# Queries of two batches loaded eight tokens to a partition, turned with the key tile, and ordered by VectorE

## The chip, the cores and the metric

One Trainium2 chip; the program runs on one of its cores. The metric is the time of one execution on the device, in microseconds, and the median over several runs is compared. Times inside an execution come from one profiled execution, counted from its first instruction.

## What is computed

Attention over four batches of eight heads with 768 tokens of 64 numbers, and after it a two-layer network. Each token attends to the tokens less than 16 away, and to 24 summaries, one for each block of 32 tokens: the key of a summary is the maximum over the block, its value the mean.

```python
k_sum = k.reshape(B, H, nb, block, D).max(axis=3)
v_sum = v.reshape(B, H, nb, block, D).mean(axis=3)
scores_l = scale * np.matmul(q, k.transpose(0, 1, 3, 2))
mask_l = np.abs(pos[:, None] - pos[None, :]) < window
scores_s = scale * np.einsum('bhsd,bhnd->bhsn', q, k_sum) + np.log(block)
...
out_a = np.matmul(softmax(concat(masked scores_l, scores_s)), concat(v, v_sum))
x = out_a as (3072 tokens, 512)
h = x @ w_in
return (h * sigmoid(beta * h)) @ w_out          # 512 -> 2048 -> 512
```

## The kernel before

**Stages.** The four batches are worked one after another, batch 0 in a way of its own. For a batch b from 1 on there are two stages. In the H stage sixteen steps (`h_tile`, L516) compute the hidden layer: `w_in` by the attention's output `xT`, 384 columns a matmul (L509), SiLU on ScalarE (L521) into `h_sb`. In the O stage six output tiles of 128 tokens are computed in four atoms each (`o_atom`, L534; matmuls L526) into the PSUM tiles `one[0]` and `one[1]` in turn; VectorE copies a finished tile to `o_sb` (`o_out`, L529) and SyncE stores it. While batch b is in its H stage, keys, queries and values of batch n = b + 1 are brought in; while it is in its O stage, the attention of batch n is computed between the atoms.

**Order.** Nothing plans the order: `run` (L551) calls the steps of a stage, and after each step those entries of a list whose position (a number of steps) has been reached. Each engine, and SyncE with its DMAs, does what it was given strictly in this order, so a waiting instruction holds up all behind it on that engine.

**How a batch comes in (L724 to L743).** Heads go in pairs, g = 0 to 3. Keys: loaded in the O stage before by `key_load` (L94) as 96 rows of two heads by eight tokens, so that a packet has 8 x 64 x 4 bytes = 2 KB; cast to bf16 by `key_cast` (L480), on GpSimd for pairs 0 and 2, on VectorE for 1 and 3; turned by a DMA transpose on SyncE's queue (`kq_dma`, L487) into `kT[g]`, where the tokens then lie as 8 blocks of 96, token 8r + c at column 96c + r; `windows_perm` (L223, two VectorE copies recorded at L247) cuts the overlapping windows of 96 tokens out of it into `kw[g]`, in the right order; `key_max_win` (L232) takes the block maxima, and `key_sums` (L240, GpSimd) spreads them over the windows. After that nothing reads `kT[g]` until the next batch's keys.

Queries: loaded by `hw_load` (L89) as 128 rows of two heads by six tokens that lie 128 apart, so that a packet has 64 x 4 = 256 bytes; cast by GpSimd (`kq_cast`, L472); turned by `kq_dma` into `qn[g]`, in order at once. Values: `load_v` (L101), 256 bytes a packet, cast by `v_cast` (L343) and half of them moved to other partitions by DMA (`v_odd_dma`, L354).

In the O stage `scores` (L323) multiplies `kw` and `qn` (L328), two halves of 384 queries for each pair; ScalarE takes the exponential (L335); VectorE masks it (`mask_e`, L337); `vm_all` (L384) sums the blocks of values in `one[0]` (L388) between the second and the third output tile; `av_mm` (L406) applies the weights to the values. `UNITS` (L721) gives the places: the scores of pair 0 and of the first half of pair 1 after the second atom, three more units after the sixth, pair 3 after the twelfth.

**Positions in the H stage.** Query loads at 0 and 0.1 for pairs 0 and 1, 0.7 and 1.7 for 2 and 3; key cast and turn at 0.5 + g and 0.6 + g; windows and maxima at 3.5 + g; query casts at 4.7 + g; query turns at 6.6 + 1.5g; spreads at 8 + g; values' casts at 12.6 + 1.2g. Casted keys and casted queries have four buffers each (tags `kn` and `qn` of the pool `nat`).

Of the kernel before, what the change touches and what calls it, by code (L numbers as in the profile page):

```python
# [11 lines left out]
def kernel(  # L12
# [10 lines left out]
    nc = tc.nc  # L23
    ctx.enter_context(tc.manual_schedule())
    P = 128
    f32 = mybir.dt.float32
    bf16 = mybir.dt.bfloat16
# [4 lines left out]
    B, H, S, D = q.shape  # L32
# [7 lines left out]
    J6 = S // P  # L40
# [4 lines left out]
    CK = 8  # L45
    RK = S // CK
# [11 lines left out]
    stage = ctx.enter_context(tc.tile_pool(name="stage", bufs=4))  # L58
    natp = ctx.enter_context(tc.tile_pool(name="nat", bufs=4))
# [10 lines left out]
    def pair(a, b, g):  # L70
        return a[b, 2 * g:2 * g + 2]


    stg = {}
# [11 lines left out]
    def sw_load(t, src, b, lo, hi):  # L86
        return nc.gpsimd.dma_start(out=row_view(t, b, lo, hi), in_=src[b, lo:hi].rearrange("h (p c) d -> p h (c d)", c=CS[b]))  # L87

    def hw_load(nm, src, b, g):  # L89
        f = stage.tile([P, 2, J6, D], f32, name=nm + "st", tag=nm + "st")  # L90
        stg[(nm, b, g)] = f
        nc.sync.dma_start(out=f[:], in_=pair(src, b, g).rearrange("h (j p) d -> p h j d", p=P))

    def key_load(b, g):  # L94
        f = stage.tile([RK, 2, CK * D], f32, name="kst", tag="kst")
        stg[("k", b, g)] = f
        nc.sync.dma_start(out=f[:], in_=pair(k, b, g).rearrange("h (p c) d -> p h (c d)", c=CK))

    vst = [const.tile([P, JV, D], f32, name=f"vst{g}") for g in range(G)]

    def load_v(b, g):  # L101
        src = pair(v, b, g).rearrange("h (j p) d -> p (h j) d", p=P)
        i = nc.sync.dma_start(out=vst[g][W:P, 0:JV - 1], in_=src[0:P - W])
        nc.sync.dma_start(out=vst[g][0:W, 1:JV], in_=src[P - W:P])
        return i
# [6 lines left out]
    def behind(a, b):  # L112
        tc.add_manual_dep(a.ins, b.ins.name,
                          mybir.DependencyInfo(mybir.DependencyClass.Sync, mybir.DependencyReason.DATA),
                          reason="order of loads")
# [27 lines left out]
    kT = [const.tile([P, S + 2 * W], bf16, name=f"kT{g}") for g in range(G)]  # L143
# [47 lines left out]
    qn = [const.tile([P, S], bf16, name=f"qn{g}") for g in range(G)]  # L191
# [31 lines left out]
    def windows_perm(cp, g, src, C):  # L223
        R, F, FW = S // C, QT // C, W // C
        t = kw[g][:, :, 0:NK].rearrange("p m (f c) -> p m f c", c=C)
        cs = src.ap[1][0]
        cp(t[:, 1:NT - 1], strided(src[:, :, F - FW:], [[F, NT - 2], [1, F + 2 * FW], [cs, C]]))
        e = kw[g][:, 0, W:NK]
        cp(strided(e, [[(NT - 1) * P - W, 2], [C, F + FW], [1, C]]),
           strided(src[:, :, 0:1], [[R - F - FW, 2], [1, F + FW], [cs, C]]))  # L230

    def key_max_win(g):  # L232
        nc.vector.tensor_reduce(out=km[g][:, NK:NK + nb].rearrange("p (m n) -> p m n", n=2),  # L233
                                in_=kw[g][:, :, W:W + QT].rearrange("p m (n f) -> p m n f", f=block), op=ALU.max, axis=AX.X)
# [5 lines left out]
    def key_sums(eng, g):  # L240
        eng.tensor_copy(out=kw[g][:, :, NK:NK + nb], in_=km[g][:, None, NK:NK + nb].to_broadcast([P, NT, nb]))  # L241
# [42 lines left out]
    def km_pe(g, ks):  # L284
        key_max_win(g)
        key_sums(ks, g)
# [56 lines left out]
    def v_cast(eng, g, lo=0, hi=JV):  # L343
        eng.tensor_copy(out=ve[:, g, lo:hi, 0:D], in_=vst[g][:, lo:hi])  # L344
# [9 lines left out]
    def v_odd_dma(g):  # L354
        nc.sync.dma_start(out=vo[0:QT, g, :, :], in_=ve[QT:P, g, :, :])
        nc.sync.dma_start(out=vo[QT:NK, g, 0:JV - 1, :], in_=ve[0:2 * W, g, 1:JV, :])
# [112 lines left out]

    nat = {}  # L470

    def kq_cast(eng, nm, b, g):  # L472
        t = natp.tile([P, J6, 2, D], bf16, name=nm + "n", tag=nm + "n")
        nat[(nm, b, g)] = t
        return eng.tensor_copy(out=t[:], in_=stg[(nm, b, g)].rearrange("p h j d -> p j h d"))  # L475

    last_mask = {}
    KC = [nc.gpsimd, nc.vector, nc.gpsimd, nc.vector]

    def key_cast(n, g):  # L480
        t = natp.tile([RK, CK, 2, D], bf16, name="kn", tag="kn")
        nat[("k", n, g)] = t
        i = KC[g].tensor_copy(out=t[:], in_=stg[("k", n, g)].rearrange("p h (c d) -> p c h d", c=CK))  # L483
        if g == 0 and n - 1 in last_mask:
            behind(i, last_mask[n - 1])

    def kq_dma(nm, b, g):  # L487
        t = kT[g][:, 0:S] if nm == "k" else qn[g][:]
        nc.sync.dma_start_transpose(out=t.rearrange("p (j t) -> p j t", j=CK if nm == "k" else J6),
                                    in_=nat[(nm, b, g)].rearrange("p j h d -> p (j h d)"))  # L490


    def h_begin(i, t, lo, hi):
# [57 lines left out]
    def run(main, sides):  # L551
        sides = sorted(sides, key=lambda x: x[0])
        for i, f in enumerate(main):
            f()
            while sides and sides[0][0] < i + 1:
                sides.pop(0)[1]()
        for _, f in sides:
            f()
# [83 lines left out]
    s = []  # L642
    wo = []

    def scale4(p, eng=None):
        for n in range(4 * p, 4 * p + 4):
            scale_w_out(n, eng)
# [27 lines left out]
    s = [(6, lambda: scale4(1)), (12, lambda: scale4(2)), (.5, clear_kw), (14, lambda: km_pe(0, nc.gpsimd))]  # L675
# [15 lines left out]
    def x_pe2(b, g, t):  # L691
        t = t.bitcast(bf16)[:, 0, 0:S]
        x = xn[(b, g)]
        for j in range(J6):
# [3 lines left out]
    s = [(.05, exp_table), (.15, lambda: scale4(3)), (.2, lambda: km_pe(1, nc.gpsimd)),  # L698
         (.3, lambda: km_pe(2, nc.gpsimd)), (3.52, lambda: km_pe(3, nc.gpsimd))]
# [16 lines left out]
    for g in range(G):  # L716
        s.append(((3.56, 3.561, 3.562, 3.563)[g], lambda g=g: key_load(2, g)))
# [6 lines left out]
    for b in range(1, B):  # L724
        n = b + 1
        s = []
        if n < B:
            for g in range(2):
                s.append((0 + .1 * g, lambda g=g, n=n: hw_load("q", q, n, g)))
            for g in range(G):  # L730
                s.append((.5 + g, lambda g=g: key_cast(n, g)))
                s.append((.6 + g, lambda g=g: kq_dma("k", n, g)))
                s.append((3.5 + g, lambda g=g: windows_perm(dve_cp, g, kT[g][:, 0:S].rearrange("p (c r) -> p c r", c=CK), CK)))
                s.append((3.6 + g, lambda g=g: key_max_win(g)))
                s.append((4.7 + g, lambda g=g: kq_cast(nc.gpsimd, "q", n, g)))
                s.append((8 + g, lambda g=g: key_sums(nc.gpsimd, g)))
                s.append((6.6 + 1.5 * g, lambda g=g: kq_dma("q", n, g)))
                s.append((12.6 + 1.2 * g, lambda g=g: v_cast(nc.gpsimd, g)))
                s.append((12.7 + 1.2 * g, lambda g=g: v_odd_dma(g)))
            for g in range(2):  # L740
                s.append((.7 + g, lambda g=g, n=n: hw_load("q", q, n, g + 2)))
                s.append((2.7 + g, lambda g=g: load_v(n, g)))
                s.append((6.7 + 1.5 * g, lambda g=g: load_v(n, g + 2)))  # L743
        if n + 1 < B:
            for g in range(G):
                s.append(((16.31, 16.32, 19.3, 19.31)[g], lambda g=g, n=n: key_load(n + 1, g)))
        late = [x for x in s if x[0] >= 16]
        run([lambda i=i: h_tile(b, i) for i in range(k2)], [x for x in s if x[0] < 16])
        s = [((x[0] - 16) * 1.2, x[1]) for x in late]
        if n < B:  # L750
            for j, (g, u, bg, pos, late) in enumerate(UNITS):
                s.append((pos + .01 * j, lambda n=n, g=g, u=u, bg=bg: scores(n, g, u, bg)))
                if g < G - 1:
                    s.append((late, lambda n=n, g=g, u=u: mask_e(n, g, u)))
            s.append((.05, exp_table))
            s.append((11.19, silu_table))
            av_at(n, s, [11.2, 14.1, 14.2, 14.3], [0, 1, 2, 0])
            for g in range(G):
                s.append(((11.3, 14.35, 14.4, 14.5)[g], lambda g=g: x_dma(n, g)))
            s.append((5.89, lambda: vm_all(one[0], [dve_cp] * 4)))  # L760
            s.append((8.3, lambda: spread(0)))
            s.append((8.31, lambda: spread(1)))
        main = [lambda ms=ms, a=a: o_atom(b, ms, a) for ms in range(J6 - (n == B)) for a in range(4)]
        run(main, s)
        if n == B:
            ms = J6 - 1
            for lo, hi in ((0, 256), (256, 512)):
                t = one[0 if lo else 1][:, 0]
                for kk in range(k2):
                    o_mm(ms, kk, t, lo, hi)  # L770
                o = op.tile([P, hi - lo], f32, name="o_half", tag=f"o_half{lo}", bufs=1)
                nc.vector.tensor_copy(out=o[:], in_=t[:, 0:hi - lo])
                nc.sync.dma_start(out=out_r[b * J6 + ms][:, lo:hi], in_=o[:])
# [29 lines left out]
```

## Time and profile before

| | us |
|---|---|
| median of 3 runs | 215.21 (214.99 to 216.19) |
| profiled execution | 215.1 |
| its span, first to last instruction | 213.2 |
| TensorE busy in it | 205.9 |
| VectorE, ScalarE, GpSimd busy | 109.9, 106.8, 53.8 |
| H stage of batch 1 | 76.1 to 97.1 |
| O stage of batch 1 | 97.1 to 122.2 |
| H stage of batch 2 | 122.2 to 143.0 |
| O stage of batch 2 | 143.0 to 168.2 |

The profiled execution's time is 1.9 us more than its span, for what lies before the first and after the last instruction. In the page, a row of forty digits shows the span in equal slices of 5.33 us, a digit being the busy share in tenths. The chain of waits is followed back from the last instruction, at each step to what released it; a row is start, length, engine, tile and line. A timeline row is start, length, engine, line, operation, output and inputs with their shapes, how many, and in square brackets how long the engine had been idle and what ended that. A row of the groups has, after the bar, busy time in all, mean ns of one, and after the second bar the idle time before them. A row of the windows has the stretch, its length, busy time and number of instructions for TensorE's matmuls, its weight loads, VectorE, ScalarE and GpSimd, and at the end the granted TensorE clock, the share of the DMA engines (over 1 where packets overlap) and GB/s. SyncE's queue is SPq; its lengths are those of the issue, and the landing comes later.

### The profile page before, as it was taken

How to read it: one execution, taken by the hardware profiler on the slowest of the kernel's cores; microseconds unless marked ns; L12 is line 12 of the kernel's file. 1: busy time of each engine (PE TensorE's matmuls, PEld its weight loads, DVE VectorE, ACT ScalarE, POOL GpSimd, SP SyncE). 2: the span in 40 equal slices, each digit the busy share in tenths (PEclk: the TensorE clock that was granted, in tenths of full speed). 3: DMA queues.
4: the chain of work that ended last, by engine and by line, in shares of the span. 5: the costliest groups of instructions: out<-in, count | busy, mean ns of one | idle time of the engine just before them, and what ended most of it. 6: DMA issues, size and time to landing. Idle time of an engine off the chain costs nothing.

```text
span 213.2 us, 5296 instructions
## 1 busy us (share of the span) xinstructions
PE 205.9 (97%) x2238; PEld 120.9 (57%) x2238; DVE 109.9 (52%) x252; ACT 106.8 (50%) x141; POOL 53.8 (25%) x85
## 2 busy tenths in 40 slices
PE   7879999999999999999999999999999999999993
PEld 7667766665445555565555466654554555554452
DVE  5567686298857723951898216644887100002121
ACT  2448785686767018669541057777450086640000
POOL 7947990002421203642003013443000000000000
PEclk9999999999999999999999999999999999999999
DMA  6999999999969989999579999999445500001212
GB/s 120 196 209 160 187 201 195 199 207 196 202 174 240 246 208 229 221 212 168 113 222 284 199 191 235 157 200 205 128 133 118 145 0 0 0 3 49 98 52 96
DMA packets 74534, 34.08 MB, mean 160 GB/s; under 512 B 61440, under 2 KB 70032, under 8 KB 74512
## 3 DMA queue, kind: packets, MB, share of 16 engines
q1 hardware_dynamic: 57440, 24.05, 53.4%
q0 software_dynamic: 7440, 7.34, 21.6%
q10 hardware_dynamic: 9632, 2.37, 7.6%
q8 instruction: 17, 0.28, 0.6%
q14 instruction: 5, 0.04, 0.1%
HBM read 27.37 MB, written 6.29 MB: 158 GB/s over the span
## 4 chain that ended last, share of the span: by engine, by line
PE 91%; DMA 3%; DVE 2%; POOL 1%; issue 1%; POOLq 0%; DVEq 0%
PE one L526 39%; PE big L509 29%; PE big L495 5%; PE one L501 3%; DMA qrow<-in_q_dram 3%; PE big L414 2%; PE big L328 2%; DVE qn L247 2%; PE big L501 2%; PE big L276 1%; PE big L315 1%; PE big L307 1%; PE one L388 1%; POOL krow L87 1%; PE big L260 1%
## 5 line engine op out<-in xcount | busy, mean ns | idle before, releaser
L526 PE MATMUL one<-w_out_sb,h_sb 128*128 128x512 bf16 (+1 forms) x400 | 85.8, 371 | 0.0
L521 ACT ACTIVATE h_sb<-big,beta_sb 128x768 bf16<-128x768 f32 x48 | 42.7, 901 | 48.0 <-PE big L509 48.0
L509 PE MATMUL big<-xT,w_in_sb 128*128 128x384 bf16 x384 | 63.1, 326 | 0.0
L526 PEld LDWEIGHTS <-h_sb 128*128 128x128 bf16 x400 | 38.0, 98 | 41.3 <-issue 0.2
L509 PEld LDWEIGHTS <-w_in_sb 128*128 128x128 bf16 x384 | 37.6, 98 | 25.3 <-issue 0.2
L247 DVE COPY o_sb<-one 128x512 f32<-128x512 f32 x19 | 13.1, 689 | 45.2 <-PE one L526 45.1
L335 ACT ACTIVATE e<-big,bias 128x768 bf16<-128x768 f32 x32 | 26.7, 898 | 15.8 <-PE big L328 13.7
L339 DVE TENSOR_TENSOR e<-e,mask 128x768 bf16<-128x768 bf16 x27 | 15.4, 596 | 13.6 <-ACT e L335 13.5
L247 DVE COPY kw<-kT 128x960 bf16<-128x960 bf16 (+1 forms) x16 | 10.3, 685 | 15.1 <-DMA kT<-kn 15.1
L344 POOL CAST ve<-vst 128x832 bf16<-128x832 f32 x15 | 13.5, 906 | 9.8 <-DMA vst<-in_v_dram 7.7
L475 POOL CAST qn<-qst 128x768 bf16<-128x768 f32 x8 | 6.6, 828 | 32.1 <-DMA qst<-in_q_dram 32.1
L241 POOL COPY kw<-km 128x288 bf16<-128x288 bf16 x12 | 6.9, 581 | 25.6 <-DVE km L233 25.6
L441 DVE TENSOR_TENSOR xn<-big,r 128x768 bf16<-128x768 f32 (+1 forms) x13 | 12.0, 927 | 0.4
L495 PE MATMUL big<-xT,w_in_sb 128*128 128x384 bf16 x64 | 11.6, 327 | 0.0
L233 DVE TENSOR_REDUCE km<-kw 128x24 bf16<-128x768 bf16 x12 | 11.3, 948 | 0.3
L640 ACT ACTIVATE h_sb<-big,beta_sb 128x384 bf16<-128x384 f32 x16 | 8.1, 581 | 3.1 <-PE big L495 3.1
L483 POOL CAST kn<-kst 96x1024 bf16<-96x1024 f32 x4 | 4.2, 1040 | 20.3 <-DVE e L339 19.3
L543 PE MATMUL one<-blank 128*128 128x128 bf16 (+1 forms) x105 | 7.4, 235 | 1.3 <-DVE blank L125 1.3
L501 PEld LDWEIGHTS <-w_in_sb 128*128 128x128 bf16 x64 | 6.2, 98 | 4.1
L501 PE MATMUL one<-xT,w_in_sb 128*128 128x384 bf16 x44 | 8.1, 326 | 0.0
L495 PEld LDWEIGHTS <-w_in_sb 128*128 128x128 bf16 x64 | 5.8, 98 | 3.4
L503 ACT ACTIVATE h_sb<-one,beta_sb 128x384 bf16<-128x384 f32 x11 | 6.4, 582 | 2.2 <-PE one L501 1.7
(126 smaller groups left out, 186.1 us busy)
## 6 DMA issues: line engine op xcount, KB each, us to landing
out_dram<-o_sb SPq DMA_DIRECT2D x23, 256.0 KB, 2.8
vst<-in_v_dram SPq DMA_DIRECT2D x13, 336.0 KB, 4.9
kst<-in_k_dram SPq DMA_DIRECT2D x8, 384.0 KB, 5.5
qst<-in_q_dram SPq DMA_DIRECT2D x8, 384.0 KB, 4.2
w_in_sb<-in_moe_w_in_dram POOLq DMA_DIRECT2D x4, 512.0 KB, 6.0
w_out_sb<-in_moe_w_out_dram POOLq DMA_DIRECT2D x4, 512.0 KB, 12.7
vo<-ve SPq DMA_DIRECT2D x12, 107.2 KB, 2.3
vst<-in_v_dram SPq DMA_DIRECT2D x3, 416.0 KB, 6.3
```

The costliest lines, as they stand in the source:

```text
L233: nc.vector.tensor_reduce(out=km[g][:, NK:NK + nb].rearrange("p (m n) -> p m n", n=2), in_=kw[g][:, :, W:W + QT].rearrange("p m (n f) -> p ...
L247: nc.vector.tensor_copy(out=o, in_=i)
L335: return nc.scalar.activation(out=e[:], in_=s[:, :, 0:HS], func=ACTF.Exp, bias=bias[:, 0:1], scale=scale)
L339: return nc.vector.tensor_mul(out=e.rearrange("p h (m q) -> p h m q", q=QT), in0=e.rearrange("p h (m q) -> p h m q", q=QT), in1=mask[:, No ...
L344: eng.tensor_copy(out=ve[:, g, lo:hi, 0:D], in_=vst[g][:, lo:hi])
L441: nc.vector.tensor_mul(out=x[:, 3 * us[0]:3 * us[0] + 3 * n].rearrange("p (k j) h d -> p k (j h) d", k=n), in0=tv[:, :, :, 0:D], in1=r[:, ...
L495: nc.tensor.matmul(t[:, 0:HS], w_in_sb[:, ki, i * P:(i + 1) * P], xT[:, ki, 0:HS], start=(ki == 0), stop=(ki == k1 - 1))
L501: nc.tensor.matmul(t[:, 0:HS], w_in_sb[:, ki, i * P:(i + 1) * P], xT[:, ki, lo:lo + HS], start=(ki == 0), stop=(ki == k1 - 1))
L509: nc.tensor.matmul(t[:, kk, 0:HS], w_in_sb[:, ki, i * P:(i + 1) * P], xT[:, ki, kk * HS:(kk + 1) * HS], start=(ki == 0), stop=(ki == k1 - 1))
L521: nc.scalar.activation(out=h_sb[:, i, :].rearrange("p (k m) -> p k m", k=2), in_=t[:, :, 0:HS], func=ACTF.Silu, scale=beta_sb[:, i:i + 1])
L526: nc.tensor.matmul(t[:, 0:hi - lo], h_sb[:, n, ms * P:(ms + 1) * P], w_out_sb[:, n, lo:hi], start=(n == 0), stop=(n == k2 - 1))
L640: nc.scalar.activation(out=h_sb[:, i, 0:HS], in_=t[:, i % 2, 0:HS], func=ACTF.Silu, scale=beta_sb[:, i:i + 1])
```

## The change

Batches 2 and 3 load their queries in the form of the keys: 96 rows, eight neighbouring tokens to a row, 2 KB a packet. The query cast has the keys' shape too (96 x 1024), and casted keys and queries share one set of four buffers (tag `rn`). The turn of the queries goes into `kT[g]`, the tile of the keys, after `windows_perm` has copied the windows out of it. New is `q_order`: two VectorE copies for each pair, a half of the rows each, bring the queries from `kT[g]` in token order into `qn[g]`, at positions 10.4 + 1.5g of the H stage; on VectorE they come after the last `key_max_win` and ahead of the first `mask_e` of the O stage. All other positions and the code of batches 0 and 1 stay.

```diff
-    def hw_load(nm, src, b, g):
-        f = stage.tile([P, 2, J6, D], f32, name=nm + "st", tag=nm + "st")
+    def row_load(nm, src, b, g):
+        f = stage.tile([RK, 2, CK * D], f32, name=nm + "st", tag=nm + "st")
         stg[(nm, b, g)] = f
-        nc.sync.dma_start(out=f[:], in_=pair(src, b, g).rearrange("h (j p) d -> p h j d", p=P))
+        nc.sync.dma_start(out=f[:], in_=pair(src, b, g).rearrange("h (p c) d -> p h (c d)", c=CK))
...
-    def kq_cast(eng, nm, b, g):
-        t = natp.tile([P, J6, 2, D], bf16, name=nm + "n", tag=nm + "n")
+    def row_cast(eng, nm, b, g):
+        t = natp.tile([RK, CK, 2, D], bf16, name=nm + "n", tag="rn")
         nat[(nm, b, g)] = t
-        return eng.tensor_copy(out=t[:], in_=stg[(nm, b, g)].rearrange("p h j d -> p j h d"))
+        return eng.tensor_copy(out=t[:], in_=stg[(nm, b, g)].rearrange("p h (c d) -> p c h d", c=CK))
...
-    def kq_dma(nm, b, g):
-        t = kT[g][:, 0:S] if nm == "k" else qn[g][:]
-        nc.sync.dma_start_transpose(out=t.rearrange("p (j t) -> p j t", j=CK if nm == "k" else J6),
+    def row_dma(nm, b, g):
+        nc.sync.dma_start_transpose(out=kT[g][:, 0:S].rearrange("p (j t) -> p j t", j=CK),
                                     in_=nat[(nm, b, g)].rearrange("p j h d -> p (j h d)"))
+
+    def q_order(g):
+        out, src = qn[g].rearrange("p (r c) -> p r c", c=CK), kT[g][:, 0:S].rearrange("p (c r) -> p r c", c=CK)
+        for r in (slice(0, RK // 2), slice(RK // 2, RK)):
+            nc.vector.tensor_copy(out=out[:, r], in_=src[:, r])
...
-                s.append((4.7 + g, lambda g=g: kq_cast(nc.gpsimd, "q", n, g)))
+                s.append((4.7 + g, lambda g=g: row_cast(nc.gpsimd, "q", n, g)))
                 s.append((8 + g, lambda g=g: key_sums(nc.gpsimd, g)))
-                s.append((6.6 + 1.5 * g, lambda g=g: kq_dma("q", n, g)))
+                s.append((6.6 + 1.5 * g, lambda g=g: row_dma("q", n, g)))
+                s.append((10.4 + 1.5 * g, lambda g=g: q_order(g)))
```

`key_load` and `key_cast` call `row_load` and `row_cast` with unchanged work. `RK` is 96, `CK` 8, `J6` 6, `P` 128.

## The prediction

> **What bounds the kernel now.** I read the page first (busy shares, the forty slices), then the chain of waits, then the timeline around the place where the queries are used, then the DMA queue and the windows.
>
> ```profile
> PE 205.9 (97%) x2238; PEld 120.9 (57%) x2238; DVE 109.9 (52%) x252; ACT 106.8 (50%) x141; POOL 53.8 (25%) x85
> PE   7879999999999999999999999999999999999993
> DMA  6999999999969989999579999999445500001212
> ```
>
> TensorE is busy in every slice but the first few and the last, at the full clock, and so are the 16 DMA engines from 80 to 100 us, where batch 2 is brought in. The chain of waits for that stage:
>
> ```profile
> 97.08 1.73 PE one L526 x8
> 98.81 0.63 PE big L328 x36
> 99.44 3.56 PE one L526 x16
> 103.00 0.51 PE one L388 x28
> 103.51 0.63 PE big L328 x36
> ```
>
> Every piece is TensorE and each begins where the last ended; from 55.9 us to 209.7 the whole chain is like this. So nothing that only shortens a transfer can shorten this kernel; the change can only leave the time as it is or put a wait into this row. The chain names where the queries of batch 2 are needed: pairs 0 and 1 at 98.81 (L328, the scores), pairs 1 and 2 at 103.51, pair 3 at 109.43. Batch 3 is the same 45.93 us later (its L388 begins at 148.93).
>
> What else stands at 103.00: L388 (the block sums of the values) writes the PSUM tile from which the first output tile must have been copied.
>
> ```profile
> 100.36 0.56 DVE L339 TENSOR_TENSOR e<-e,mask 128x768 bf16<-128x768 bf16 x1 [6.54 <-ACT e L335]
> 101.15 0.92 DVE L339 TENSOR_TENSOR e<-e,mask 128x768 bf16<-128x768 bf16 x1 [0.23 <-ACT e L335]
> 101.99 0.68 DVE L247 COPY o_sb<-one 128x512 f32<-128x512 f32 x1
> 102.93 0.40 PEld L388 LDWEIGHTS <-A_avg 128*32 128x32 bf16 x28 [0.42 <-DVE o_sb L247]
> ```
>
> VectorE stands idle 6.54 us, masks two weight tiles, copies the output tile until 102.67, and TensorE takes it up 0.3 us later. For batch 3 the same copy ends at 148.24 and L388 follows at 148.93.
>
> **What the change adds there.** In the changed order of VectorE's instructions the eight ordering copies (two for each pair of heads) stand between the last block maximum (over by 93.8 us) and these two mask products. Engines run in order: if the copies of pairs 2 and 3 wait for their turned queries, masks and output copy wait behind them, and TensorE behind those, although it needs pair 3 only 6 us later. That is the one place where the change touches the chain.
>
> Cost of a copy: 128x384 with the source stepping 192 bytes is not in the trace. Nearest rows have the same access pattern:
>
> ```profile
> L247 DVE COPY kw<-kT 128x960 bf16<-128x960 bf16 x8 | 8.4, 1050 | 15.1 <-DMA kT<-kn 15.1
> L247 DVE COPY kw<-kT 128x160 bf16<-128x160 bf16 x8 | 2.6, 320 | 0.0
> ```
>
> The undisturbed ones took 0.98 and 0.28 us, a slope of 0.875 ns an element, hence 0.48 us for 384; consecutive ones overlap by 0.07, so 0.41 us each in a row. Bounds: 0.35 us (the 128x384 copies out of PSUM, 352 ns) and 0.60 (0.48 by 1250/980, the slowest 960 against an undisturbed one). I take 0.41: four copies are 1.7 us, eight are 3.3 us a batch, 6.6 us on VectorE in all, which is idle half the span; only what follows the last landing can reach the path.
>
> When do the turned queries land? The DMA queue:
>
> ```profile
> 90.43 1.21 SPq L489 DMA_TRANSPOSE qn<-qn  x1
> 93.08 1.34 SPq L489 DMA_TRANSPOSE qn<-qn  x1
> 96.09 3.73 SPq L489 DMA_TRANSPOSE qn<-qn  x2
> ```
>
> Pair 2 is issued at 96.09 and lands 5.0 us later, 101.1; pair 3 lands at 101.8. In batch 3: 143.41 plus 4.3, 147.7, and 148.4. With landings as they are, the copies end 1.7 us after pair 2: 102.8. Two masks at 0.46 us (two took 0.92 together above) and the output copy of 0.68 put the tile's release at 104.4 against the 103.0 that TensorE wants: 1.4 us lost. Batch 3: 147.7+1.7+1.6=151.0 against 148.9: 2.1 us. So without any relief 3.5 us.
>
> GpSimd is busy there too. It casts the last value tile (L344, 0.88 us) as soon as that lands, at 100.67 in this profile, 0.4 us before pair 2's landing, so it runs until 0.4 after. Do the two engines disturb each other?
>
> ```profile
> 88.64 1.79 POOL L241 COPY kw<-km 128x288 bf16<-128x288 bf16 x2
> 88.68 1.46 DVE L247 COPY kw<-kT 128x960 bf16<-128x960 bf16 x2 [0.33 <-DMA kT<-kn]
> ```
>
> The GpSimd copies take 0.43 us each alone; here the second ran until 90.43, just after VectorE's two copies (of this same strided kind) ended at 90.14, and those took 1.46 instead of 1.19. So they exclude each other in good part. Ends: 0, or the whole 0.4 us; I take 0.2, which makes the losses without relief 1.6 and 2.3 us. The Trainium skill, "SBUF — State Buffer", in its terms under the shared port pair, has VectorE's two-port copies and GpSimd hold it as a lock for a whole instruction, the loser fully blocking, which speaks against this change; these rows roughly agree, and by it alone the losses without relief would be 1.8 and 2.5.
>
> **What the change relieves.** Eight query loads of 384 KB go from 1,536 packets of 256 B each to 192 of 2 KB. The turns keep their bytes (192 KB of bf16 each). How fast either kind moves:
>
> ```profile
> 80.00:98.00 18.00, 17.98 (x110) 10.65 (x109) 9.38 (x13) 13.21 (x15) 8.44 (x11) 1.00 1.31 219
> 66.00:68.00 2.00, 2.00 (x11) 0.93 (x10) 1.93 (x5) 1.69 (x3) 0.00 (x0) 1.00 0.97 230
> 68.00:70.00 2.00, 2.00 (x77) 1.43 (x75) 0.91 (x3) 0.59 (x1) 1.52 (x2) 1.00 1.07 311
> 110.00:112.00 2.00, 2.00 (x32) 1.07 (x27) 1.97 (x4) 1.98 (x3) 0.00 (x0) 1.00 1.01 313
> ```
>
> The last two columns are the DMA engines' share and GB/s. The first window is the saturated stage of 256 B packets: 219 GB/s. The others are stretches of key loads and output stores, 2 KB packets: 230 at worst, 311 to 313 when nothing stalls. Four query loads (1.57 MB) take 7.2 us at 219; 5.05 at 311, 6.8 at 230. The relief to everything queued behind them is 2.1 us at best and 0.3 at worst; since the first two loads meet a queue not yet full (share 1.06 in 78 to 80 us), I take 1.8, nearer to the two undisturbed windows. The Trainium skill, "DMA: Bandwidth & Descriptors", section "Why small descriptors are slow (HBM only)", gives a fixed 3 cycles on each 256-byte descriptor's 8; worked out from that, an estimate, 2 KB needs 67 cycles where eight small ones need 88, and the relief would be 1.7 us.
>
> Does the queue let it through? SyncE issues the loads, turns and value loads in one row without a break from 77.25 to 98.6 us. The shortest turn there holds it 1.21 us, a load 0.45 to 0.58; the first turns took 2.47, 1.82 and 1.59 since they were held back by the full engines. At the short durations pair 2's turn could be issued at about 93, 3 us earlier, so SyncE hides in the relief.
>
> Sum: batch 2 loses 1.6-1.8, nothing; batch 3 loses 2.3-1.8=0.5. Profiled execution 215.1 us (span 213.2) plus 0.5 is 215.6; the median of the runs is 215.2, so 215.7 on that footing.
>
> **The rest, at nothing, and its cover.** The query casts go from 0.83 us (L475) to the 1.04 of the key casts (L483, same tile shape): 0.21 by 8 on GpSimd, 25% busy. They now share four buffers with the keys, so each waits for the turned key of its pair: pair 3 for 91.45 us instead of its load at 87.8. Behind it in GpSimd's order stand four spreads of the block maxima (L241, 0.43 each) and the value casts; they end at about 94.4, as now, since the last maximum is only ready at 93.8. The scores need them at 98.81: 4.4 us of cover. The turns of the queries now write the key tile and wait until the windows are copied from it: 84.8, 87.4, 90.1, 92.8 against issues at 90.4, 93.1, 96.1, 97.4, and the relief moves both. The next batch's key turns wait for the ordering copies, 25 us earlier. The first batches run unchanged instructions.
>
> **Rivals.** (1) Slower: relief too small, the convoy shows. The 2 KB packets beside turns move like the 230 GB/s window, relief 0.3 us: 1.3+2.0=3.3 us, 218.5. Half-way, relief 1.2: 0.4+1.1=1.5, 216.7. It decides from a relief under about 1.4 us, where the loss passes 1.1. For it: the window at 66 us and a place so narrow (0.3 to 0.7 us of room). Against it: 311 and 313 GB/s. (2) Slower: the shared buffers hold up GpSimd. If pair 3's turned key lands more than 4.4 us later than now, the spreads come after 98.81, and a microsecond more costs one per batch: some 217. Against it: the key turns get earlier, not later. (3) Faster: TensorE gains from a quieter memory, say 1 ns of 162 per matmul of the three later stages, 1.2 us: 214.0. Nothing speaks for it; the clock column is 1.00 and the matmuls are back to back. (4) The packets do not get longer: then (1) at no relief, 3.5 to 4.3 us; the key loads already have this very form, so it stays within (1).
>
> **Chances.** Forecast (loss 0 to 1.1) 0.52; rival 1 0.39; rival 2 0.06; rival 3 0.03. A difference of 0.5% (1.1 us) is what can be told from none here. So faster 0.03, same 0.52, slower 0.45. The predicted time is the forecast's 215.7. Range: down to 214.8, the spread of the runs; up to 218.3, a relief of 0.4. The forecast's own range is 214.9 to 216.3.
>
> **What would show it.** In the changed profile: VectorE's idle time in 94 to 100 us filled by pairs of 0.4 to 0.5 us copies, each pair behind a landing; pair 2's query turn landing at about 99.3 and 145.9; L388's weight load waiting on the output copy, by nothing in the first H stage and half a microsecond in the second; DMA packets down by 8 times 1,344. I am wrong if TensorE waits anywhere but at L388, if pair 2 lands no earlier than now, or if the GpSimd cast holds the ordering copies for its full length.

## The result, and the profile after

| | before | changed |
|---|---|---|
| median of 22 runs, us | 215.19 (214.15 to 216.19) | 216.68 (215.81 to 219.97) |
| ratio | | 1.0075 [1.0054, 1.0096] |
| profiled execution, us | 215.1 | 216.57 |
| its span, us | 213.2 | 214.8 |

The change costs 1.5 us, 0.75%. The ratios leave out a run more than 1.5% above the fastest of its kernel (here 219.97). The time lies in the range and beyond the half per cent of the forecast: what came is rival 1, and the half-way price that was written down for it (216.7). Lines of `kernel.py` from L104 to L480 stand two lower than before: the block sums are L386, the scores L326, the masks L337, the output copy L245; the ordering copies are L490, the casts in the keys' form L473, their turns L484.

The page of the changed kernel first: TensorE's busy time, the packets, the instruction queue (packets, MB, share), and two groups.

```profile
PE 204.9 (95%) x2221; PEld 121.1 (56%) x2238; DVE 122.3 (57%) x268; ACT 106.7 (50%) x141; POOL 57.6 (27%) x85
DMA packets 63782, 34.08 MB, mean 159 GB/s; under 512 B 49152, under 2 KB 57744, under 8 KB 63760
q8 instruction: 17, 0.28, 0.6%
L473 POOL CAST qn<-qst 96x1024 bf16<-96x1024 f32 x8 | 10.6, 1326 | 35.4 <-DMA kT<-kn 34.6
L490 DVE COPY qn<-kT 128x384 bf16<-128x384 bf16 x16 | 9.7, 656 | 5.7 <-DMA kT<-qn 5.7
```

TensorE works as long as before (205.9 then, with 17 records more) in a longer span, so it waits somewhere: its share of the span fell from 97% to 95%. The chain of waits names the place, in batch 2 and in batch 3:

```profile
94.98 5.18 DMA kT<-qn
100.16 0.02 issue
100.18 1.96 DVE qn L490 x4
102.14 0.93 DVE e L337 x2
103.07 0.61 DVE o_sb L245
103.69 0.04 issue
103.73 0.58 PE one L386 x25
...
142.77 4.24 DMA kT<-qn
...
147.03 0.88 DVE qn L490 x2
...
148.04 0.87 DVE qn L490 x2
148.91 0.93 DVE e L337 x2
149.85 0.61 DVE o_sb L245
...
150.50 0.58 PE one L386 x28
```

Read it from below: the block sums wait for the output copy, that stands behind two masks, those behind four ordering copies, and these for the turned queries of pair 2, landed at 100.16 and 147.01. Before, the chain was TensorE alone here.

How large is the wait? TensorE's own timeline has it:

```profile
98.50 0.70 PE L326 MATMUL big<-qn,kw 64*128 64x64 bf16 x36
103.73 0.58 PE L386 MATMUL one<-ve,A_avg 128*32 128x128 bf16 x28 [0.97 <-DVE o_sb L245]
```

The scores of pairs 0 and 1 begin at 98.50, the block sums at 103.73: 5.23 us, where the same stretch took 98.81 to 103.00 = 4.19 before. So 1.04 us are lost in batch 2; likewise 145.47 to 150.50 = 5.03 against 4.18 in batch 3, 0.85. Together 1.9 us. By the same timeline the O stage of batch 2 began at 96.68, and at 96.92 before (the chain of waits, which starts a piece where the last one ended, put it at 97.1): 0.24 earlier, which leaves 1.65, the 1.6 by which the span grew.

And the relief? Landings are compared from the start of their O stage, 96.92 and 142.85 before, 96.68 and 143.65 after. Pair 2 landed 4.19 and 4.87 us after it before, 3.48 and 3.36 after: relief 0.71 and 1.51 us, not 1.8. That is one profile against one. In e8 and e10 below, which load and turn the queries in the same way, pair 2 landed 3.49 and 3.79 us after the stage's start in batch 2 and 3.05 and 3.06 in batch 3: relief 0.4 to 0.7 in the one, 1.8 in the other. e6, the kernel before with more VectorE copies, has 4.75 and 5.13, so a landing moves by up to half a microsecond from profile to profile. Batch 2 is where the relief fell short. SyncE's row shows for batch 2 where it was earned and where a part went back. Start, length of the issue, line, operation; before:

```profile
78.74 2.47 SPq L489 DMA_TRANSPOSE kT<-kn  x1
81.89 1.82 SPq L489 DMA_TRANSPOSE kT<-kn  x1
84.44 1.59 SPq L489 DMA_TRANSPOSE kT<-kn  x1
86.70 0.86 SPq L104 DMA_DIRECT2D vst<-in_v_dram  x1
87.66 1.21 SPq L489 DMA_TRANSPOSE kT<-kn  x1
```

and after:

```profile
78.38 1.31 SPq L484 DMA_TRANSPOSE kT<-kn  x1
80.47 1.23 SPq L484 DMA_TRANSPOSE kT<-kn  x1
82.43 1.21 SPq L484 DMA_TRANSPOSE kT<-kn  x1
84.32 1.94 SPq L102 DMA_DIRECT2D vst<-in_v_dram  x1
86.36 1.21 SPq L484 DMA_TRANSPOSE kT<-kn  x1
```

The three key turns that stand among the query loads are issued in 3.75 us, not 5.88: the 2.1 us that were hoped for at best. But the second part of the first value load then holds SyncE for 1.94 us, not 0.86, and 1.1 us are gone again. From the fourth key turn on each round of a turn and two value loads takes 2.75, 2.80 and 3.07 us (2.77, 2.65 and 3.01 before): no query load is left in it, and nothing gets faster. Pair 2's turn is issued at 94.98, 1.1 us earlier than before, 0.9 against the start of its stage. In batch 3 the three key turns fell from 6.08 to 3.69 us. The first value load's second part was held before too (2.06 us, now 1.93); this time it is the second value load's that is held (2.08, 0.62 before), and pair 2's turn is issued 1.4 us earlier against its stage. The windows agree (the last column is GB/s, the one before it the DMA engines' share); the changed kernel, and then the one before:

```profile
79.00:81.00 2.00, 1.99 (x13) 1.10 (x12) 0.00 (x0) 2.00 (x3) 0.00 (x0) 1.00 0.96 301
81.00:83.00 2.00, 2.00 (x14) 1.19 (x13) 0.51 (x1) 1.60 (x3) 0.39 (x1) 1.00 1.09 249
83.00:85.00 2.00, 2.00 (x15) 1.19 (x13) 2.00 (x3) 1.38 (x2) 1.40 (x1) 1.00 1.24 246
85.00:87.00 2.00, 2.00 (x14) 1.22 (x13) 2.00 (x3) 1.42 (x2) 1.04 (x1) 1.00 1.15 230
98.00:99.00 1.00, 1.00 (x37) 0.58 (x37) 0.21 (x1) 1.00 (x1) 0.00 (x0) 1.00 0.14 13
```

```profile
81.00:83.00 2.00, 2.00 (x14) 1.22 (x13) 0.00 (x0) 1.60 (x3) 0.94 (x2) 1.00 1.32 216
83.00:85.00 2.00, 2.00 (x14) 1.22 (x13) 1.41 (x3) 1.60 (x2) 0.71 (x1) 1.00 1.31 235
85.00:87.00 2.00, 2.00 (x14) 1.17 (x12) 2.00 (x3) 1.20 (x3) 0.83 (x1) 1.00 1.28 241
```

The first pairs of loads run at 301 GB/s (260 in the same two microseconds before). As soon as more turns, and then value loads, are in the queue it is 249, 246, 230 (216, 235, 241 before). The last row of the changed kernel is a halt, spoken of at the end.

### The profile page after: what moved, and what is told of

Its sections match the earlier page's. It is cut to its first block, busy times and chain, and to the rows that moved or that the text cites. A ratio compares the mean times of both kernels' runs of the same rounds, so it can differ in the third digit from the quotient of the medians.

```text
span 214.8 us, 5288 instructions
## 1 busy us (share of the span) xinstructions
PE 204.9 (95%) x2221; PEld 121.1 (56%) x2238; DVE 122.3 (57%) x268; ACT 106.7 (50%) x141; POOL 57.6 (27%) x85
## 2 busy tenths in 40 slices
DMA packets 63782, 34.08 MB, mean 159 GB/s; under 512 B 49152, under 2 KB 57744, under 8 KB 63760
## 4 chain that ended last, share of the span: by engine, by line
PE 62%; DMA 17%; DVE 13%; issue 3%; POOL 2%; SPq 2%; POOLq 0%; DVEq 0%
PE one L526 30%; PE big L509 18%; DMA vst<-in_v_dram 6%; PE big L495 5%; DVE kw L245 5%; DMA kT<-qn 4%; DMA kT<-kn 4%; PE big L412 2%; DMA qrow<-in_q_dram 2%; DVE km L231 2%; DVE qn L490 2%; DVE w_out_sb L214 2%; PE big L326 2%; PE one L501 1%; DVE o_sb L245 1%
## 5 line engine op out<-in xcount | busy, mean ns | idle before, releaser
L526 PE MATMUL one<-w_out_sb,h_sb 128*128 128x512 bf16 (+1 forms) x383 | 83.4, 371 | 1.9 <-issue 1.4
L245 DVE COPY o_sb<-one 128x512 f32<-128x512 f32 x19 | 13.1, 689 | 45.2 <-PE one L526 45.0
L245 DVE COPY kw<-kT 128x960 bf16<-128x960 bf16 (+1 forms) x16 | 14.4, 944 | 11.4 <-DMA kT<-kn 11.4
L473 POOL CAST qn<-qst 96x1024 bf16<-96x1024 f32 x8 | 10.6, 1326 | 35.4 <-DMA kT<-kn 34.6
L342 POOL CAST ve<-vst 128x832 bf16<-128x832 f32 x15 | 14.3, 970 | 7.3 <-DMA vst<-in_v_dram 6.3
L337 DVE TENSOR_TENSOR e<-e,mask 128x768 bf16<-128x768 bf16 x27 | 14.5, 566 | 2.0 <-ACT e L333 1.9
L490 DVE COPY qn<-kT 128x384 bf16<-128x384 bf16 x16 | 9.7, 656 | 5.7 <-DMA kT<-qn 5.7
L239 POOL COPY kw<-km 128x288 bf16<-128x288 bf16 x12 | 6.1, 522 | 21.0 <-DVE km L231 20.1
L473 POOL CAST kn<-kst 96x1024 bf16<-96x1024 f32 x4 | 4.0, 1037 | 20.6 <-DVE e L337 20.6
```

The costliest lines, as they stand in the source:

```text
L245: nc.vector.tensor_copy(out=o, in_=i)
L337: return nc.vector.tensor_mul(out=e.rearrange("p h (m q) -> p h m q", q=QT), in0=e.rearrange("p h (m q) -> p h m q", q=QT), in1=mask[:, No ...
L490: nc.vector.tensor_copy(out=out[:, r], in_=src[:, r])
L526: nc.tensor.matmul(t[:, 0:hi - lo], h_sb[:, n, ms * P:(ms + 1) * P], w_out_sb[:, n, lo:hi], start=(n == 0), stop=(n == k2 - 1))
```

## The experiments

All are the changed kernel with one edit, except e6, which starts from the kernel before, e7 with two edits, and e10 with none. Ratios are against the kernel before on the same chip. "Loss" is the time from the start of the scores of pairs 0 and 1 to the block sums, less the 4.19 (batch 2) or 4.18 (batch 3) of before.

**Is it the place of the copies?** e1 moves the ordering copies of pairs 2 and 3 behind the output copy, e2 those of pair 3 alone.

```diff
-                s.append((10.4 + 1.5 * g, lambda g=g: q_order(g)))
+                if g < 2:
+                    s.append((10.4 + 1.5 * g, lambda g=g: q_order(g)))
...
+            s.append((3.9, lambda: q_order(2)))
+            s.append((6.5, lambda: q_order(3)))
```

In e2 the condition is `g < 3` and only the last line is added.

> The ordering copies of pairs 2 and 3 move into the O stage: pair 2 to just behind the copy of the first output tile, pair 3 to after the seventh atom. Theory A (convoy: the two mask products and the output copy queue on VectorE behind copies that wait for landings, and L388 waits for them): nothing waits any more, the 0.9 to 1.0 us lost at L388 in each of the two O stages goes, ratio to before 0.999 to 1.002. Rival B (the copies cost by being there: VectorE time, or the lock-step with GpSimd's casts): the same copies still run, ratio stays at 1.006 to 1.009.

> Only the ordering copies of pair 3 move, to after the seventh atom; pair 2 stays ahead of the masks. Theory A: what stands behind pair 2's landing is now one pair of copies (0.9 us) instead of two; in the changed kernel's trace the output copy would end 0.8 us earlier, at 102.9 where L388 wants it at 102.75, so 0.1 to 0.2 us is lost in the first O stage and about nothing in the second: ratio 1.000 to 1.003. Rival B: ratio 1.006 to 1.009.

| | ratio | loss, batch 2 | batch 3 |
|---|---|---|---|
| changed | 1.0075 [1.0054, 1.0096] | 1.04 | 0.85 |
| e1, pairs 2 and 3 later | 0.9997 [0.9975, 1.0018] | 0 | 0 |
| e2, pair 3 later | 1.0002 [0.9982, 1.0023] | 0.34 | 0.12 |

The chain of waits of e1, and VectorE's timeline at the same place:

```profile
98.11 0.63 PE big L326 x36
98.74 1.62 PE one L526 x7
100.36 0.05 issue
100.41 1.89 PE one L526 x8
102.30 0.51 PE one L386 x28
```

```profile
100.93 0.68 DVE L245 COPY o_sb<-one 128x512 f32<-128x512 f32 x1
101.53 0.88 DVE L490 COPY qn<-kT 128x384 bf16<-128x384 bf16 x2
102.31 0.56 DVE L337 TENSOR_TENSOR e<-e,mask 128x768 bf16<-128x768 bf16 x1
```

The output copy goes first, pair 2's copies follow it in the 0.8 us before the next mask, and the chain is TensorE's again. The loads, casts, turns and copies are all still there; only the copies' place on VectorE differs. So the loss is that place. e2 stands between in its profile, as it should: without pair 3's two copies (0.9 us) there is 0.34 and 0.12 left of 1.04 and 0.85; its ratio is not to be told from that of e1.

**Is it the copies' work?** e6 gives the kernel before eight copies of the same form at the same places, from `kT` to a tile that nobody reads, waiting for no landing.

```diff
+    spare = [qrow[:, g * 1024:g * 1024 + S] for g in range(G)]
+
+    def idle_copies(g):
+        out, src = spare[g].rearrange("p (r c) -> p r c", c=CK), kT[g][:, 0:S].rearrange("p (c r) -> p r c", c=CK)
+        for r in (slice(0, RK // 2), slice(RK // 2, RK)):
+            nc.vector.tensor_copy(out=out[:, r], in_=src[:, r])
...
+                s.append((10.4 + 1.5 * g, lambda g=g: idle_copies(g)))
```

> The kernel before, with eight more VectorE copies a batch of the ordering copies' form and at their places, from the key tile into a tile that nobody reads; they wait for no landing. Theory A: they run in VectorE's idle 6.5 us ahead of the masks and cost nothing, ratio 0.999 to 1.002. Rival B (VectorE's added time and its exclusion of GpSimd cost): ratio 1.004 or more, with GpSimd's value casts later and TensorE waiting at L388 or at the scores.

0.9997 [0.9974, 1.002]. VectorE's timeline:

```profile
93.85 5.57 DVE L497 COPY qrow<-kT 128x384 bf16<-128x384 bf16 x8
100.38 0.56 DVE L339 TENSOR_TENSOR e<-e,mask 128x768 bf16<-128x768 bf16 x1 [0.96 <-ACT e L335]
101.65 0.68 DVE L247 COPY o_sb<-one 128x512 f32<-128x512 f32 x1
```

Eight copies take 5.57 us beside GpSimd's casts, and VectorE still has 0.96 us to spare before the first mask. The work costs nothing that can be measured; it costs when it starts behind a late landing.

**What do the 2 KB packets give?** e3 loads the queries of the changed kernel in 256-byte packets again (a row of the tile padded from 64 to 72 numbers, so that tokens do not lie together; one load for a head, 16 loads in place of eight).

```diff
-        f = stage.tile([RK, 2, CK * D], f32, name=nm + "st", tag=nm + "st")
+            f = stage.tile([RK, 2, CK, D + 8], f32, name=nm + "st", tag=nm + "st")[:, :, :, 0:D]
...
+            for h in range(2):
+                nc.sync.dma_start(out=f[:, h], in_=src[b, 2 * g + h].rearrange("(p c) d -> p c d", c=CK))
```

> The changed kernel with its query loads in 256 B packets again (a padded tile, one load for each head, so 16 loads instead of 8 on SyncE; all else as changed). Theory A with relief from the packets: the relief of 0.7 and 1.4 us seen in the two stages is gone, so the loss per stage is what the prediction gave without relief, 1.6 and 2.3 us, together 3.9 us: ratio 1.015 to 1.020. Rival C (the relief has nothing to do with the packet size, the landings moved because of the order or the tile shape): ratio stays at 1.006 to 1.010.

1.0283 [1.0246, 1.0319], more than was expected; there are 74,662 packets again. The edit changes two things: the packets, and the number of query loads, which hold SyncE for 5.3 us in batch 2 where they took 2.2 in the changed kernel. Its profiled execution (223.47, the median is 221.14) had lost 3.6 us in batch 0 already, where the granted clock was 0.91 from 20 to 40 us (1.00 in the changed kernel), so its landings are read from the start of the O stage. Pair 2 landed 4.83 us after it in batch 2, against 3.48 in the changed kernel and 4.19 before; in batch 3 5.30, against 3.36 and 4.87. The losses are 2.3 and 2.7 us, 1.0 of the second already inside the scores, which wait for pair 1 there. The prediction's losses without relief, 1.6 and 2.3, with the 0.64 and 0.43 by which pair 2 lands later than before, give 2.2 and 2.7. (The ratio is worth 6.1 us; 1.1 of them lie outside these two losses and were not placed.) The chain in batch 3:

```profile
149.65 4.23 DMA kT<-qn
...
153.91 1.82 DVE qn L496 x4
...
157.32 0.58 PE one L392 x28
```

It is the chain of the changed kernel, only later: what the landing loses, TensorE loses. With the loads in their old form the relief is gone, so rival C is out; but how much of the 1.35 and 1.94 us between e3's landings and the changed kernel's is due to the packets, and how much to the longer issue on SyncE, was not separated.

**Can the loads gain more if they go together?** e4 puts the query loads of pairs 2 and 3 ahead of the first key turn; e7 does this and also moves the fourth key cast ahead of the first window copies; e8 moves that cast alone.

```diff
-                s.append((.7 + g, lambda g=g, n=n: row_load("q", q, n, g + 2)))
+                s.append((.2 + .1 * g, lambda g=g, n=n: row_load("q", q, n, g + 2)))
...
-                s.append((.5 + g, lambda g=g: key_cast(n, g)))
+                s.append(((.5, 1.5, 2.5, 3.4)[g], lambda g=g: key_cast(n, g)))
```

> The changed kernel with the query loads of pairs 2 and 3 issued right behind those of pairs 0 and 1, ahead of the first key turn. Theory D (2 KB packets run at 300 GB/s among themselves but at 230 to 246 beside turns, as the changed kernel's windows read): four loads together take some 1 us less of the DMA engines, the turned queries of pair 2 land 0.5 to 1 us earlier than in the changed kernel, and the loss at L388 shrinks from 1.9 us to 0.3 to 0.9: ratio 1.002 to 1.005. Rival E (the place of the loads is nothing to the DMA engines, all is a matter of bytes): pair 2 lands as in the changed kernel, ratio 1.006 to 1.009; if the key turns, now later, hold up what follows, 1.009 or more.

1.0346 [1.03, 1.0392]: worse than any other version. SyncE's row, and VectorE's:

```profile
79.16 6.46 SPq L484 DMA_TRANSPOSE kT<-kn  x3
...
86.30 0.68 SPq L102 DMA_DIRECT2D vst<-in_v_dram  x1
89.85 1.22 SPq L484 DMA_TRANSPOSE kT<-kn  x1
```

```profile
86.33 2.04 DVE L245 COPY kw<-kT 128x960 bf16<-128x960 bf16 x2 [9.03 <-DMA kT<-kn]
88.28 1.54 DVE L473 CAST kn<-kst 96x1024 bf16<-96x1024 f32 x1
```

SyncE stands from 87.0 to 89.85. Its next instruction, the fourth key turn, waits for the fourth key cast, which VectorE does behind the first window copies, and these wait for the first key turn, which now lands at 86.31 (82.46 in the changed kernel) behind four loads. A convoy again, one step up. Of what was expected only the last clause came, key turns that hold up what follows.

> As the run with the four query loads together, and the fourth key cast ahead of the first window copies on VectorE, so that the fourth key turn no longer waits for the first one's landing. Theory D (2 KB loads move faster when they are not beside turns): the queue does not stand still, pair 2 lands 0.5 us or more earlier than in the changed kernel, ratio 1.002 to 1.006. Theory G (bytes and packets behind one another cost the same in any order; what the loads gain among themselves the later stretch gives back): pair 2 lands as in the changed kernel, ratio 1.006 to 1.010. Both expect it far below the 1.035 of the run without the moved cast, whose loss they put down to SyncE's 2.8 us at the fourth key turn.

> The changed kernel with the fourth key cast ahead of the first window copies, nothing else. In the changed kernel's trace the fourth key turn was issued behind a value load that the full DMA engines held for 1.9 us, after the cast was done; so theory A expects no change: ratio 1.005 to 1.010. If the cast did hold the queue (rival F's second half), 1.002 to 1.005.

e8 is the changed kernel over again (1.0112 [1.0077, 1.0147], losses 1.05 and 0.57; the changed kernel beside it had 1.0097 [1.0078, 1.0117]). In e7 the queue no longer stands, the fourth key turn goes out at 86.12, and yet it is 1.0227 [1.0189, 1.0264], which neither theory had. Pair 1 lands 0.45 us before the O stage, no earlier than in the changed kernel (0.52): the three key turns are held for 6.19 us in all, where theirs took 3.75. So with the loads together the landings gain nothing; the held time only moves from one instruction to another. Pair 2 lands 2.40 us after the stage's start, 1.1 sooner; the halt that comes before it in the changed kernel came after it here. That was no help, since VectorE itself was late; its timeline and then GpSimd's:

```profile
96.90 6.24 DVE L490 COPY qn<-kT 128x384 bf16<-128x384 bf16 x8
103.07 1.01 DVE L337 TENSOR_TENSOR e<-e,mask 128x768 bf16<-128x768 bf16 x2
```

```profile
97.62 4.40 POOL L342 CAST ve<-vst 128x832 bf16<-128x832 f32 x4
```

All eight copies run in a row beside four value casts: 6.24 us, where eight at the 0.44 of an undisturbed pair (0.87 for two, above) are 3.5 and four casts at 0.88 are 3.5 too. 7.0 us of work of the two engines went by in 6.24, nearly one after the other.

**Do the shared buffers cost?** e5 casts the queries into buffers of their own (slices of `qrow`, which has no other reader by then); e9 is the same kernel again, e10 the changed kernel again on e9's chip.

```diff
-        t = natp.tile([RK, CK, 2, D], bf16, name=nm + "n", tag="rn")
+        if nm == "q":
+            t = qrow[0:RK, g * 1024:(g + 1) * 1024].rearrange("p (c h d) -> p c h d", c=CK, h=2)
+        else:
+            t = natp.tile([RK, CK, 2, D], bf16, name=nm + "n", tag="rn")
```

> The changed kernel with the casted queries in the row tile of batches 0 and 1 (idle by then), not in the four buffers shared with the keys. Theory D: GpSimd casts the queries as they land, before the windows are cut, so VectorE's window copies take 1.0 us again and not up to 2.1, but the turns wait for the DMA engines and not for casts, so pair 2 lands as in the changed kernel and the ratio stays at 1.006 to 1.009. Rival F (the shared buffers cost half the relief: casts and window copies exclude each other, the fourth key cast and turn and all behind it come late): pair 2 lands 0.5 us or more earlier, ratio 1.002 to 1.005.

> The run with own buffers for the casted queries once more, beside the changed kernel on the same chip. In its trace all 16 DMA engines stood twice for about a microsecond between 95 and 100 us, in the changed kernel's once. Theory H (that second halt is chance): ratio as the changed kernel's, within 0.4%. Rival I (own buffers are really slower): 0.4% or more above the changed kernel, with the same two halts in the trace.

> The changed kernel unaltered, beside the others on the same chip: ratio 1.005 to 1.010, TensorE waiting at L388 about 1 us in each of the two O stages, pair 2 of batch 2 landing 3.2 to 3.8 us after the O stage begins.

e5 1.013 [1.0082, 1.0177], e9 1.0166 [1.0128, 1.0204], e10 1.0097 [1.0078, 1.0117]. Buffers of their own gain nothing, so rival F is out; they look slower, and why, the profiles do not settle. Pair 2 lands 5.11 us after the stage's start in e5 and 4.00 in e9, against 3.48 in the changed kernel and 3.79 in e10, and the first loss is 2.38 and 1.27 against 1.04 and 1.17. So e5's profile is slower at the known place, but e9's loses only 0.1 us a batch more there than e10's, and 0.5 us at 76 us waiting for `xT`, far from the edit. In both, the DMA engines falter around 95 us, while pair 2's turn is on its way: from 95 to 96 us they moved 49 GB/s in e9 and 116 in e5, and 247 in e10. Part of the gap goes with the clock: three of e9's six runs (218.63 to 219.47 us) had a granted clock of 0.992; the other three, at 0.997 and more, took 216.92 to 217.59, and e10's at such a clock 216.19 to 216.96. Without the runs at 0.992 the medians are 217.16 and 216.7, which is 0.2% and not 0.7. Whether own buffers bring the halt or the lower clock stays open.

No version beat the kernel before: it is bound by TensorE, and the best that a version did (e1) is to give the loss back.

## Why the prediction was right or wrong

- **The bound and the place: right.** TensorE waits at L386 for the output copy, 1.0 and 0.8 us, and but for gaps of 0.2 us nowhere else in the two O stages; e1 removes the loss by moving VectorE instructions alone, e6 shows that the copies' work is covered.
- **The convoy's formula: right.** It gave losses of 1.6 and 2.3 us without relief. With the relief that came, 0.71 and 1.51, it gives 0.9 and 0.8; measured 1.04 and 0.85. e3, e8 and e10, whose pair 2 lands at other times, agree within 0.2 us (1.2 and 0.5 for e10, measured 1.17 and 0.58). The four copies were put at 1.7 us and 0.2 for GpSimd: 1.96 and 1.88 us from the first copy's start to the masks.
- **The relief: the step that failed.** It was taken as 1.8 us, "nearer to the two undisturbed windows" of 311 and 313 GB/s. It was 0.71 and 1.51 in the changed kernel's profile, 0.4 to 0.7 and 1.8 in e8 and e10: near enough for batch 3, mis-sized for batch 2, which was to lose nothing and lost 1.04. Only the first loads met such a stretch (301 GB/s); the others ran among turns and value loads at 230 to 249, about the 230 of the window at 66 us that was taken as the lower end. The step that let it through, "so SyncE hides in the relief", reckoned that pair 2's turn could be issued 3 us earlier, and it was 1.1. It saw that the turns' issues would shrink, and they did, by 2.1 us; it overlooked that the next value load would be held in their place (1.94 us), and that from the fourth key turn on SyncE has no query load left, so that its rounds of 2.8 to 3.1 us stay. (SyncE's row before ends at 99.8, not at 98.6 as was read: the last turn holds it for 2.40 us. Nothing hangs on that.) The Trainium skill, "DMA: Bandwidth & Descriptors", section "Why small descriptors are slow (HBM only)", was worked out to an estimate of 1.7; it prices the packets and not the queue they stand in. The traces gave 0.4 to 0.7 in batch 2 and 1.5 to 1.8 in batch 3.
- **Rival 1 came, at its half-way price.** It was to decide below a relief of about 1.4 us; the two reliefs average 1.1, and 216.7 was worked out for 1.2. That it meets the median of 216.68 so closely is luck: the losses of the profile are 1.9 us, less 0.24 by which a stage began earlier. The chance of 0.39 against the forecast's 0.52 was the wrong way round, and the rows at hand could not have settled it: 230, 311 and 313 are all stretches of key loads and output stores, and none had long packets among key turns and value loads.
- **GpSimd beside the copies: right in kind.** A copy took 656 ns in the mean against the 410 to 480 expected, and GpSimd works beside most of them; undisturbed pairs took 0.44 us a copy. Those behind pair 2's landing, which alone count, met the last value cast as it ended, and the 0.2 us was enough. The Trainium skill, "SBUF — State Buffer", section "Who interferes with whom", says that VectorE in a two-port mode and GpSimd block each other for a whole instruction. That these copies run in such a mode no run here shows, but e7 comes near it (7.0 us of work in 6.24).
- **Shared buffers: right, for a reason left out.** Rival 2 did not come: the spreads end at 94.9 (94.4 was predicted), the scores start at 98.5. That each query cast waits for the turned key of its pair was foreseen. Not foreseen: VectorE starts that pair's window copies at the same moment, so the two meet: casts of 1326 ns instead of 1040, window copies of 1205 and 682 instead of 1050 and 320. e5 and e9 keep them apart (window copies of 1090 and 348 in e5) and gain nothing by it.
- **Packets: exact.** 74,534 to 63,782 is 10,752, 8 times 1,344. Rival 4 is out. Rival 3 is out too: with the wait moved away e1 is at 0.9997.

## What to carry to other kernels

When an engine works in order, a copy that waits for a transfer costs what stands behind it, not what it does: put it behind the instruction that the bound engine needs next, as e1 does, and only then ask how late the transfer may be. A transfer's gain is to be priced at the rate of the mixture that it runs in, and only while the queue that issues it still has such transfers; the time that one instruction no longer stands may be the time that the next one does. And where TensorE bounds the stage, as here, earlier landings can at best take such a loss away.

## What the runs showed of the hardware that was not expected

- **Halts of the DMA engines.** For about a microsecond nearly nothing moves: 13 GB/s at 98 to 99 us in the changed kernel, 22 at 99 to 100 in the kernel before. The traces of these two have four such halts each amid the traffic (5 to 22 GB/s), and each begins towards the end of one packet of the instruction queue, or just behind it (17 packets, 0.28 MB, so 16 KB each), that itself took 1.0 to 1.4 us. That the packet is the cause was not tested. The extra halts of e5 and e9 near 96 us follow an 8 KB packet of a second instruction queue, which the changed kernel has too, at 96.3 us, with no halt behind it. In e7, where the halt fell behind pair 2's landing and not ahead of it, pair 2 landed 1.1 us sooner after the stage's start: as much as the change's whole relief.
- **A strided copy and a GpSimd cast take turns, nearly.** Eight copies that need 3.5 us took 5.57 (e6) and 6.24 (e7) beside GpSimd's work.
- **Long packets in a mixed queue gained little.** From 81 to 87 us the DMA engines moved 242 GB/s with the queries in 2 KB packets and 231 with 256 bytes, in both beside turns and value loads of 256 bytes; in the two microseconds before, 301 and 260.
